# Folding a norm's scale into the QKV weights, reordering the prologue and keying the output projection per tile, in a statically ordered transformer block

## The chip, the cores and the metric

The kernel runs on one core of a Trainium2 chip. The metric is the device time of one execution in microseconds (us). "Faster" or "slower" is given at 2%; differences below that are told with their 95% intervals.

Ratios are the mean time of one kernel's fast runs over that of the kernel before in the same rounds, so they are not quite the ratio of the medians that stand beside them. The experiments ran in three batches (e; f, g and p; c), each with its own runs of the kernel before; between batches it is safer to compare ratios than times.

## The reference, cut to what matters

One transformer block with adaptive layer norms: 2048 tokens, width 1024, 32 query heads of width 32 that share one key and one value head, and a gated feed-forward of width 3584, all in bf16.

```python
mod = (silu(c) @ w_mod).reshape(1, 6, 1, -1)
sa, ca, ga, sb, cb, gb = ...                 # shift, scale, gate of both halves
h = layernorm(x) * (1 + ca) + sa
q = (h @ wq).reshape(heads); k = h @ wk; v = h @ wv        # one k and v for all heads
x = x + ga * (softmax(q @ k.T / sqrt(32)) @ v) @ wo
h = layernorm(x) * (1 + cb) + sb
x = x + gb * (silu(h @ w1) * (h @ w3)) @ w2
```

## The kernel before

The program is a graph of small nodes. A scheduler on the host lays it out with a simple model of durations: at each step it takes the engine that can start first and gives it the ready node of best priority. What goes to the chip is a fixed order for each engine, with semaphores (counters on which one engine waits for another) between the engines. The program has no means of changing this order while it runs. That a group of matmuls is "keyed on" a tile means that it is made to wait for that tile.

The order on TensorE in words: scores (class S) go first, since they feed the exponentials on ScalarE; the products with V and the sums of the denominators (V, D) come next; the rest (class F: projections, feed-forward) fills what is left; it is called filler below.

```python
# Dag.schedule (cut): the choice on TensorE
def key(c):
    s, n = c
    if n.cls == "S":
        r = 0
    elif n.cls is not None:
        r = 1 if att or t - n.est > 1.0 else 4
    else:
        r = 3
    return (r, n.prio, n.seq)
...
st = max(dma_free, s + 1.2)             # the model of a load
dma_free = st + n.nbytes / 300e3
n.vis = dma_free + 0.8
```

Matmuls write into PSUM, from which VectorE or ScalarE must copy the result before the place can be used again (the copy is called eviction). The eight PSUM banks are two general ones (PB) and a ring of six for the scores (SP). The front works in four groups of 512 tokens; each is normalised, transposed on TensorE and evicted with scale and shift, and then gives keys, values and, for the first group, queries:

```python
# ln_transpose (cut): eviction needs the modulation MODC, so all of w_mod's first part must be in
G.add("act", lambda e, ...: e.activation(dst(c), PBH[g.bank][...], ACT.Identity,
      scale=MODC[:, fm, c:c + 1], bias=MODC[:, fs, c:c + 1]), ...)
...
for tb in range(NTB):
    for i in range(4):
        ln_stats(tb * 4 + i)
    ln_scale(tb * 4, 4)
    ...
    ln_transpose(4, q0, ..., 0, 1, ("act", "dve") if tb < 2 else ("dve",))
    kv(tb)                       # keys and values of 512 tokens
    if tb == 0:
        qproj(0, 0)
```

After that come eight blocks of 256 queries, numbered from 0: 128 exponentials of 128x1024 each, then `post`: output projection WO, second norm, and feed-forward. The feed-forward of block b fills TensorE while the scores of block b+1 run.

```python
def post(q0, qn):                # one block: two tiles of 128 tokens
    for i in range(nt):
        t = t0 + i
        for h in range(2):       # WO; keyed on BOTH tiles of QT (qkeys(f, q0, qn))
            g = mm_group(NC, ..., lambda f, s=s: qkeys(f, q0, qn) + [("WOG", f), ("X", s)], prio=4)
            ...
        ln_stats(t, s); ln_scale(t, 1); ln_norm(t, i, s)
        dma(lambda e, t=t, i=i: e.dma_start_transpose(QT[:, :, t * P:(t + 1) * P], xnt(i)), ...)
    for c in range(NC):          # modulate on VectorE
        G.add("dve", lambda e, c=c: e.tensor_scalar(QT[:, c, q0:q0 + qn], ..., ALU.mult, ALU.add), ...)
    # feed-forward: 448 matmuls of 256 columns for w1, w3 and 224 for w2
```

The DMA transpose of the first tile writes that tile's part of QT. Since WO of the second tile is keyed on both tiles, it waits for that transpose, which it does not need.

The softmax here doesn't subtract the row's maximum and nothing guards it: scores larger than these inputs give would overflow.

Of the kernel before, what the change touches and what calls it, by code (L numbers as in the profile page):

```python
# [3 lines left out]
BF16 = mybir.dt.bfloat16  # L4
# [15 lines left out]
class Group:  # L20
    def __init__(self):
        self.bank = None
        self.nodes = []


class Dag:
# [76 lines left out]
    def schedule(self, banks):  # L103
# [41 lines left out]
        while left:  # L145
            best = None
            for e in ENGS:
                if not ready[e]:
                    continue
                tf = t_free[e]  # L150
                fb = free_banks() if e == "pe" else None
                cands = []
                tmin = None
                for n in ready[e]:
                    est = n.est
                    if n.acq is not None:
                        if not fb:
                            continue
                        est = max(est, fb[0][0] + SEM_LAT)
                    if n.cls == "S":  # L160
                        idle = [bank_idle(b) for b in n.sbanks if b not in closed]
                        if any(x is None for x in idle):
                            continue
                        est = max([est] + [x + SEM_LAT for x in idle if x])
                    s = max(tf, est)
                    cands.append((s, n))
                    if tmin is None or s < tmin:
                        tmin = s
                if not cands:
                    continue  # L170
                if best is None or tmin < best[0]:
                    best = (tmin, e, cands)
# [29 lines left out]
            if n.acq is not None:  # L202
                fb = free_banks()
                b = fb[0][1]
                old = bank_group[b]
                if old is not None:
                    for x in old.nodes:
                        if x.eng != "pe":
                            n.deps.append(x)
                bank_group[b] = n.acq  # L210
                n.acq.bank = b
# [19 lines left out]
            if n.dsem is not None:  # L231
                st = max(dma_free, s + 1.2)
                dma_free = st + n.nbytes / 300e3
# [101 lines left out]
def build(nc, x_in, wq_in, wk_in, wv_in, wo_in, w1_in, w3_in, w2_in, c_in, wmod_in, out, S, D, F):  # L335
# [14 lines left out]
    NXS = 8  # L350

# [12 lines left out]
    NG = 2  # L364
    TP = -1
# [17 lines left out]
    RS = sb("RS", [P, NT], F32)  # L383
    NHALF = sb("NHALF", [P, 4], F32)
# [16 lines left out]
    WKK, WVK = [("QT", NC - 1, S - 512), ("QT", NC - 1, S - 384)], [("QT", NC - 1, S - 256), ("QT", NC - 1, S - 128)]  # L401
    SCBK = [("QT", a, S - 512 + b) for a in range(NC // 4) for b in range(0, 512, P)]
# [14 lines left out]
    def grp():  # L417
        return Group()
# [27 lines left out]

    xload(0, 8)
    for k in range(NC):
        dma(lambda e, k=k: e.dma_start(WM01[:, k, :], wmod_in[k * P:(k + 1) * P, 0:2 * D]), ("wm01", k),
            writes=[("UR", k)], nbytes=P * 2 * D * 2)  # L450
    dma(lambda e: e.dma_start(WKV[:, 0], wk_in.rearrange("(c p) f -> p c f", p=P)), "wk", writes=WKK, nbytes=65536)
    dma(lambda e: e.dma_start(WKV[:, 1], wv_in.rearrange("(c p) f -> p c f", p=P)), "wv", writes=WVK, nbytes=65536)
    WQK = [("WREG", "q")]
    dma(lambda e: e.dma_start(WQ[:, :, 0:P], wq_in[:, 0:P].rearrange("(c p) f -> p c f", p=P)), "wq0",
        writes=[("WQ", 0)] + WQK, nbytes=P * D * 2)


    G.add("act", lambda e: e.activation(CT[:], CROW[:], ACT.Tanh, scale=0.5), reads=["CROW"], writes=["CT"], dur=0.25)
    G.add("dve", lambda e: e.scalar_tensor_tensor(CT[:], CT[:], 1.0, CROW[:], ALU.add, ALU.mult),
# [13 lines left out]
    g = grp()  # L473
    for k in range(NC):
        def mm(e, k=k, g=g):
            for j in range(16):
                i = e.matmul(PB[g.bank][:, j:j + 1], WM01[:, k, j * P:(j + 1) * P], SCT[:, k:k + 1],
                             start=(k == 0 and j == 0), stop=True, skip_group_check=True)
            return i
        G.add("pe", mm, reads=["SCT", ("UR", k)], dur=16 * 0.06, lat=0.2, acq=g if k == 0 else None,  # L480
              groups=[(g, "w")], mode="F")
    G.add("dve", lambda e, g=g: e.tensor_copy(MODC[:, 0, :], PB[g.bank][:, 0:8]), writes=[("MODC", 0)],
          groups=[(g, "r")], dur=0.13, prio=0)
    G.add("dve", lambda e, g=g: e.tensor_scalar(MODC[:, 1, :], PB[g.bank][:, 8:16], 1.0, None, ALU.add),
          writes=[("MODC", 1)], groups=[(g, "r")], dur=0.13, prio=0)
    G.add("pool", lambda e: e.tensor_copy(WKR[:], WKV[:, 0].unsqueeze(2).broadcast_to([P, NC, 4, 32])), reads=WKK,
          writes=["WKR"], dur=1.3)

    def ln_stats(t, s=None):
        s, q = t % NXS if s is None else s, t % 4  # L490
        for a in range(2):
# [3 lines left out]
              reads=[("ST", q, 0), ("ST", q, 1)], writes=[("MV", t)], dur=0.15, prio=2)  # L495

# [20 lines left out]
    def ln_transpose(nt, q0, dst, dkeys, fs, fm, engs, prio=5):  # L517
# [3 lines left out]
        for cb in range(NC // ncb):  # L521
            g = grp()
# [9 lines left out]
            for h in range(ncb):  # L532
                c = cb * ncb + h
                en = engs[cb % len(engs)]
                if en == "act":
# [12 lines left out]
    def mm_group(n, f, reads_f, n_cols=512, per=1, prio=5, late=0):  # L548

        g = grp()  # L550
        for i0 in range(0, n, per):
            def run(e, i0=i0, g=g):
                for i in range(i0, min(n, i0 + per)):
# [5 lines left out]
                  groups=[(g, "w")], mode="F", prio=prio)  # L559
        return g  # L560

    def kv(tb):
        sl = slice(tb * 512, (tb + 1) * 512)
        hk = lambda c: [("HT", c, tb), HKEY]
        g = mm_group(NC, lambda e, b, c: e.matmul(b, WKR[:, c].rearrange("p a f -> p (a f)"), HT[:, c, sl],  # L565
                                                  start=c == 0, stop=c == NC - 1), lambda c: ["WKR"] + hk(c))
        G.add("dve", lambda e, g=g: e.tensor_copy(KT[:, sl], PB[g.bank]), writes=[("KT", tb)], groups=[(g, "r")],
              dur=dve_t(512), prio=1)

        def vmm(e, b, i):  # L570
# [3 lines left out]
        g = mm_group(4 * NC, vmm, lambda i: WVK + hk(i % NC), n_cols=128, per=NC)  # L574
        G.add("dve", lambda e, g=g: e.tensor_copy(V[:, tb * 4:tb * 4 + 4, :].rearrange("p t f -> p (t f)"),
                                                  PB[g.bank][:, 0:128]),
              writes=[("V", tb)], groups=[(g, "r")], dur=dve_t(128), prio=1)

    def qproj(tb, f):
        sl = slice(tb * 512, (tb + 1) * 512)  # L580
        g = mm_group(NC, lambda e, b, c: e.matmul(b, WQ[:, c, f * P:(f + 1) * P], HT[:, c, sl],  # L581
                                                  start=c == 0, stop=c == NC - 1),
                     lambda c: [("WQ", min(f, 1)), ("HT", c, tb), HKEY] + WQK)
        G.add("dve", lambda e, g=g: e.tensor_copy(QT[:, f, sl], PB[g.bank]),
              writes=qkeys(f, tb * 512, 512), groups=[(g, "r")], dur=dve_t(512), prio=1)
# [4 lines left out]
    for tb in range(NTB):  # L590
        for i in range(4):
            ln_stats(tb * 4 + i)
        ln_scale(tb * 4, 4)
        q0 = 4 if tb == 1 else 0
        for i in range(4):
            ln_norm(tb * 4 + i, q0 + i)
        if tb + 2 < NTB:
            xl = xload(tb * 4 + 8, 4)
        ln_transpose(4, q0, lambda c, tb=tb: HT[:, c, tb * 512:(tb + 1) * 512],
                     lambda c, tb=tb: [("HT", c, tb)], 0, 1, ("act", "dve") if tb < 2 else ("dve",))  # L600
        kv(tb)
        if tb == 0:
            qproj(0, 0)
    dma(lambda e: e.dma_start(WQ[:, :, P:D], wq_in[:, P:D].rearrange("(c p) f -> p c f", p=P)), "wq1",
        reads=[("WQ", 0)], writes=[("WQ", 1)], nbytes=7 * P * D * 2, after=xl)
    wo_load = dma(lambda e: e.dma_start(WO[:], wo_in.rearrange("(c p) f -> p c f", p=P)), "wo", writes=["WO"],
                  nbytes=D * D * 2, after=xl)
    for f in range(1, NC):
        qproj(0, f)
# [58 lines left out]
    for tb in range(1, NTB):  # L668
        for f in range(NC):
            qproj(tb, f)  # L670
# [5 lines left out]
    def attention(q0, qn):  # L676
# [5 lines left out]
        for f in range(NC):  # L682
            pend = []
            trs = []
            for s in range(ns):
# [19 lines left out]
                G.add("pe", smm, reads=sorted({("KT", kt // 4) for kt in kts}) + qkeys(f, q0, qn),  # L705
# [91 lines left out]
    WKEYS = [("WMS", i) for i in range(3)] + WQK + [("WQ", 0), ("WQ", 1)]  # L797
# [17 lines left out]
    def post(q0, qn):  # L815
        t0, nt = q0 // P, qn // P
        xs = lambda t: t % 4
        G.chain = 1
# [3 lines left out]
        for i in range(nt):  # L822
            t = t0 + i
            s = xs(t)
            for h in range(2):
                g = mm_group(NC, lambda e, b, f, t=t, h=h: e.matmul(  # L826
                    b, QT[:, f, t * P:(t + 1) * P], WO[:, f, h * 512:(h + 1) * 512], start=f == 0,
                    stop=f == NC - 1), lambda f, s=s: qkeys(f, q0, qn) + [("WOG", f), ("X", s)], prio=4)
# [6 lines left out]
            dma(lambda e, t=t, i=i: e.dma_start_transpose(QT[:, :, t * P:(t + 1) * P], xnt(i)), ("xt", i),  # L835
                reads=[("XN", i)], writes=[("QT", c, t * P) for c in range(NC)], nbytes=P * D * 2 * 2)
        for c in range(NC):
            G.add("dve", lambda e, c=c: e.tensor_scalar(  # L838
                QT[:, c, q0:q0 + qn], QT[:, c, q0:q0 + qn], MODC[:, 4, c:c + 1], MODC[:, 3, c:c + 1],
                ALU.mult, ALU.add), reads=[("MODC", 3), ("MODC", 4)] + qkeys(c, q0, qn), writes=qkeys(c, q0, qn),  # L840
                dur=dve_t(qn, 4) + 0.12, prio=2)
# [128 lines left out]
```

## Time and profile before

The time before was 1196.2 us (median of 3; 1194.97 to 1197.2).

The table of windows shows how the execution falls into stages. Its columns are the window, its length, then busy time of TensorE (PE), its weight loads, VectorE (DVE), ScalarE (ACT) and GpSimd (POOL), the granted clock of TensorE, the share of DMA time and GB/s. These are the front, the middle and the end:

```profile
0.00:60.00 60.00, 32.31 (x441) 20.74 (x442) 47.70 (x104) 18.48 (x22) 9.12 (x27) 0.93 0.81 274
...
235.00:1060.00 825.00, 822.66 (x11971) 566.10 (x11969) 723.81 (x1050) 818.07 (x925) 21.36 (x24) 1.00 0.68 187
1060.00:1210.00 150.00, 121.27 (x1193) 101.67 (x1191) 64.48 (x109) 22.61 (x30) 1.58 (x4) 0.96 0.70 189
```

In the middle TensorE is idle for 2.3 us of 825, and ScalarE is busy for 99% too. In the first 60 us TensorE is idle for 27.7.

The timeline of the front (start, duration, engine, line, operation, and in brackets the idle time before it with what ended it):

```profile
20.51 0.59 PE L477 MATMUL PB<-SCT,UREG 128*128 128x1 bf16 x16 [0.97 <-DMA UREG<-in_w_mod_dram]
...
21.41 2.79 ACT L536 ACTIVATE HREG<-SP,MODC 128x512 bf16<-128x512 bf16 x4 [18.98 <-DVE MODC L484]
...
38.05 1.94 ACT L710 ACTIVATE UREG<-SP 128x1024 bf16<-128x1024 f32 x2 [4.37 <-PE SP L700]
```

ScalarE waits 19.0 us for the modulation before it can evict the first transpose. The first exponential (L710) starts at 38.05.

The timeline of the end, from WO of the last tile (L826) to the last feed-forward (L855):

```profile
1096.73 1.89 PE L826 MATMUL SP<-WO,QT 128*128 128x512 bf16 x8
...
1101.72 3.22 PE L889 MATMUL SP<-HREG 128*128 128x256 bf16 x28
...
1106.15 3.31 SPq L835 DMA_TRANSPOSE QT<-XN  x1
...
1112.26 2.14 DVE L838 TENSOR_SCALAR QT<-QT,MODC 128x256 bf16<-128x256 bf16 x8 [5.80 <-DMA QT<-XN]
1114.54 6.46 PE L855 MATMUL PB<-QT,HREG 128*128 128x256 bf16 x32 [9.61 <-DVE QT L838]
```

TensorE has run out of filler (L889, the feed-forward of block 6), waits 9.6 us, and then runs 32 matmuls in 6.46 us; later 32 take 3.49 by the chain of waits. The granted clock, by the windows, is 0.50 from 1114.5 to 1118 and 1.00 from 1121 on.

These are the feed-forward rows of the groups on TensorE in block 4, from its first exponential at 564.24 to the next block's at 691.38 (count, busy us, mean ns, idle before):

```profile
L855 PE MATMUL PB<-QT,WREG 128*128 128x256 bf16 x256 | 32.3, 273 | 0.0
...
L855 PE MATMUL PB<-QT,HREG 128*128 128x256 bf16 x128 | 16.1, 273 | 0.0
L889 PE MATMUL PB<-WREG,HREG 128*128 128x256 bf16 x105 | 14.2, 274 | 0.0
L889 PE MATMUL PB<-HREG 128*128 128x256 bf16 x65 | 8.5, 274 | 0.0
...
L855 PE MATMUL PB<-QT,X 128*128 128x256 bf16 x64 | 8.0, 273 | 0.0
L889 PE MATMUL PB<-X,HREG 128*128 128x256 bf16 x56 | 7.3, 273 | 0.0
```

Blocks are numbered from 0. The counts add up to 674, and to 672 when counted exactly from exponential to exponential. That is one whole block's feed-forward (448 + 224): per block of scores, TensorE gets one block of filler done, without idling.

### The profile page before, as it was taken

The numbers are of one execution on the slowest core, as the hardware profiler recorded it, in microseconds if no ns is written. First come the engines' busy times: TensorE is split into PE (matmuls) and PEld (weight loads), VectorE is DVE, ScalarE is ACT, GpSimd is POOL, SyncE is SP. The second block draws the span as 40 slices with busy tenths as digits, with TensorE's granted clock in tenths as the row PEclk, the third lists the DMA queues.
The fourth block names the chain that finished last, engine by engine and source line by source line (L and its number), as shares of the span: only waits on it lengthen the run. The fifth ranks groups of instructions, "written<-read, shape, count | busy, mean of one in ns | idle before, by whom it ended". The sixth has DMA issues, their size and how long they took to land.

```text
span 1195.7 us, 35104 instructions
## 1 busy us (share of the span) xinstructions
PE 1126.3 (94%) x15681; PEld 757.1 (63%) x15681; DVE 967.2 (81%) x1443; ACT 1021.1 (85%) x1146; POOL 33.7 (3%) x59
## 2 busy tenths in 40 slices
PE   4697996799999999999999999999999999999798
PEld 3343442476666776777577766776677757777687
DVE  7867877788988998898889888989889988994451
ACT  1488999999999999999999999999999999990110
POOL 2000000000010001000000000000100010000000
PEclk9898997899999999999999999999999999999899
DMA  8715007266568665866497557765786558768894
GB/s 304 246 55 177 2 7 180 62 189 167 160 174 233 169 176 139 254 197 169 131 253 198 162 157 209 217 178 142 190 239 177 166 150 248 203 166 233 213 274 130
DMA packets 387446, 212.11 MB, mean 177 GB/s; under 512 B 25824, under 2 KB 379104, under 8 KB 387296
## 3 DMA queue, kind: packets, MB, share of 16 engines
q1 hardware_dynamic: 387296, 209.87, 62.6%
q8 instruction: 123, 2.02, 0.7%
q14 instruction: 27, 0.22, 0.1%
HBM read 201.46 MB, written 4.19 MB: 172 GB/s over the span
## 4 chain that ended last, share of the span: by engine, by line
PE 83%; ACT 8%; DVE 4%; DMA 3%; SPq 1%; issue 0%; POOL 0%
PE PB L855 31%; PE SP L700 12%; PE PB L889 12%; PE PB L741 9%; ACT UREG L710 8%; PE PB L581 4%; PE PB L826 4%; PE SP L889 4%; PE SP L855 3%; PE PB L761 2%; DMA WREG<-in_w_mod_dram 1%; DMA UREG<-in_w_mod_dram 1%; DMA QT<-XN 1%; DVE ST L492 1%; DVE HREG L542 1%; PE SP L565 1%
## 5 line engine op out<-in xcount | busy, mean ns | idle before, releaser
L710 ACT ACTIVATE UREG<-SP 128x1024 bf16<-128x1024 f32 x1024 | 967.9, 1041 | 35.0 <-PE SP L700 31.2
L729 DVE TENSOR_TENSOR UREG<-UREG 128x2048 bf16<-128x2048 bf16 x256 | 311.8, 1218 | 24.8 <-ACT UREG L710 20.8
L700 PE MATMUL SP<-QT,KT 32*128 32x256 bf16 x4096 | 206.9, 277 | 25.3 <-ACT UREG L710 18.9
L724 DVE TENSOR_TENSOR UREG<-UREG 128x2048 bf16<-128x2048 bf16 x128 | 156.5, 1223 | 69.8 <-ACT UREG L710 69.0
L855 PE MATMUL PB<-QT,WREG 128*128 128x256 bf16 x1664 | 211.6, 275 | 0.4 <-DVE QT L838 0.2
L855 PEld LDWEIGHTS PB<-QT,WREG 128*128 128x128 bf16 x1664 | 153.5, 98 | 47.6 <-issue 30.7
L700 PEld LDWEIGHTS SP<-QT,KT 32*128 32x128 bf16 x4096 | 61.0, 92 | 148.2 <-ACT UREG L710 68.9
L855 PE MATMUL PB<-QT,HREG 128*128 128x256 bf16 x1088 | 139.1, 277 | 10.7 <-DVE QT L838 9.6
L741 PE MATMUL PB<-UREG,V 128*32 128x256 bf16 x4032 | 130.5, 275 | 0.5 <-ACT UREG L710 0.5
L855 PEld LDWEIGHTS PB<-QT,HREG 128*128 128x128 bf16 x1088 | 101.3, 99 | 40.9 <-issue 29.0
L741 PEld LDWEIGHTS PB<-UREG,V 128*32 128x32 bf16 x4032 | 98.3, 97 | 25.4 <-issue 18.3
L889 PE MATMUL PB<-WREG,HREG 128*128 128x256 bf16 x700 | 91.2, 273 | 0.4 <-DVE WKR L770 0.4
L864 ACT ACTIVATE GSB<-GSB 128x512 bf16<-128x512 bf16 x56 | 36.5, 652 | 62.3 <-DVE GSB L862 62.3
L889 PEld LDWEIGHTS PB<-WREG,HREG 128*128 128x128 bf16 x700 | 63.8, 98 | 23.3 <-issue 13.3
L855 PE MATMUL PB<-QT,X 128*128 128x256 bf16 x512 | 64.8, 273 | 0.0
L826 PE MATMUL PB<-WO,QT 128*128 128x512 bf16 x232 | 62.9, 396 | 1.0 <-DMA QT<-XN 0.5
L581 PE MATMUL PB<-HREG,WREG 128*128 128x512 bf16 x256 | 62.7, 381 | 0.0
L889 PE MATMUL PB<-HREG 128*128 128x256 bf16 x476 | 62.2, 273 | 0.0
L855 PEld LDWEIGHTS PB<-QT,X 128*128 128x128 bf16 x512 | 46.9, 98 | 13.2 <-issue 8.2
L864 ACT ACTIVATE WREG<-WREG 128x512 bf16<-128x512 bf16 x56 | 36.8, 657 | 21.2 <-DVE WREG L862 21.2
L889 PEld LDWEIGHTS PB<-HREG 128*128 128x128 bf16 x476 | 43.4, 98 | 14.8 <-issue 8.9
L779 DVE RECIPROCAL WKR<-WKR 128x128 f32<-128x128 f32 x48 | 44.5, 940 | 0.3
(109 smaller groups left out, 953.0 us busy)
## 6 DMA issues: line engine op xcount, KB each, us to landing
WREG<-in_B_w_dram SPq DMA_DIRECT2D x112, 512.0 KB, 5.0
HREG<-in_B_w_dram SPq DMA_DIRECT2D x74, 512.0 KB, 5.0
WREG<-in_B_w_dram SPq DMA_DIRECT2D x33, 896.0 KB, 5.2
X<-in_B_w_dram SPq DMA_DIRECT2D x38, 512.0 KB, 4.8
HREG<-in_B_w_dram SPq DMA_DIRECT2D x21, 896.0 KB, 5.1
X<-in_B_w_dram SPq DMA_DIRECT2D x10, 896.0 KB, 5.0
X<-in_A_x_dram SPq DMA_DIRECT2D x32, 256.0 KB, 4.4
WREG<-in_w_mod_dram SPq DMA_DIRECT2D x16, 512.0 KB, 5.2
```

The costliest lines, as they stand in the source:

```text
L581: g = mm_group(NC, lambda e, b, c: e.matmul(b, WQ[:, c, f * P:(f + 1) * P], HT[:, c, sl], start=c == 0, stop=c == NC - 1), lambda c: [("WQ ...
L700: r = e.matmul(SP[:, b, o:o + qn], KT[32 * gg:32 * gg + 32, kts[j] * P:(kts[j] + 1) * P], QT[32 * gg:32 * gg + 32, f, q0:q0 + qn], start=T ...
L710: G.add("act", lambda e, u=u, h0=h0, n=n, b0=b0, nb=nb: e.activation(U[:, u, h0 * W:(h0 + n) * W].rearrange("p (b w) -> p b w", b=nb), SP[ ...
L724: G.add("dve", lambda e, tr=tr, u=u, fu=first_u: e.tensor_tensor(TR[:, tr, 0:4 * W], U[:, fu, 0:4 * W], U[:, u, 0:4 * W], ALU.add), reads= ...
L729: G.add("dve", lambda e, tr=tr, u=u: e.tensor_tensor(TR[:, tr, 0:4 * W], TR[:, tr, 0:4 * W], U[:, u, 0:4 * W], ALU.add), reads=[("TR", tr) ...
L741: r = e.matmul(PB[g.bank][32 * gg:32 * gg + 32, 0:qn], V[:, kt, :], U[:, pu, (gg * npk + j) * qn:(gg * npk + j + 1) * qn], start=w0 + n == ...
L761: r = e.matmul(PB[g.bank][32 * gg:32 * gg + 32, qn:2 * qn], SEL[:, ga, gj, :], TR[:, tr, (gg * npk + j) * qn:(gg * npk + j + 1) * qn], sta ...
L779: G.add("dve", lambda e, h=h, da=da: e.reciprocal(DSB[:, da, h * 128:(h + 1) * 128], DSB[:, da, h * 128:(h + 1) * 128]), reads=[("DSB", da ...
L826: g = mm_group(NC, lambda e, b, f, t=t, h=h: e.matmul(b, QT[:, f, t * P:(t + 1) * P], WO[:, f, h * 512:(h + 1) * 512], start=f == 0, stop= ...
L855: return e.matmul(b[:, j * qn:(j + 1) * qn], w13[:, w, c, j * P:(j + 1) * P], QT[:, c, q0:q0 + qn], start=c == 0, stop=c == NC - 1)
L864: G.add("act", lambda e, b=b: e.activation(TB[b], GS[b], ACT.Tanh, scale=0.5), reads=[("GS", b)], writes=[("TB", b)], clear=alias("TB") if ...
L889: G.add("pe", lambda e, g=g, j=j, fc=fc, hf=hf, first=first, w2s=w2s: e.matmul(PB[g.bank][:, j * 256:(j + 1) * 256], HHT[:, hf * NH + fc, ...
```

## The change

The intent: evict the first transposes without waiting for the modulation, by folding the scale into the weights of Q, K and V and the shift into biases; make all keys first and values later, so that exponentials start early and do not stop; use TensorE instead of DMA for the transposes of the first and the last block; and let WO of a tile wait only for its own tile. The diff is cut and in places shortened. It also changes the model of the loads (300 to 350) and moves the statistics of two tiles to ScalarE.

```diff
-                dma_free = st + n.nbytes / 300e3
+                dma_free = st + n.nbytes / 350e3
...
+                if fs is None:                      # ln_transpose: plain copies
+                    ... e.activation(dst(c), src(), ACT.Identity) / e.tensor_copy(dst(c), src())
...
-    def kv(tb): ...                                 # keys and values together
+    def kproj(t0, n, allow=None): ...               # four column tiles, bias on eviction
+    def vproj(tb): ...
...
+    ORDER = ("w0", "w1", "w2", "w3", "x8", "x9", "w4", "x10", "x11", "w5", "w6", "w7", "q", "x12", ...)
+    ONACT = (3, 6)                                  # statistics of two tiles on ScalarE
+    tr(0, 4, None, ("act", "dve"), (2, 3, 4, 5))    # transposes of tokens 0-1535 before the modulation
+    tr(4, 4, ...); tr(8, 4, ...)
+    ... bias matmuls for Q, K, V; WKV and WQ multiplied by 1 + scale
+    kproj(0, 256, (2,)); qproj(0, 256, 0, (3,)); kproj(256, 256, (0, 1)); ...
+    tr(12, 4, None, TR3E, (0, 1)); kproj(1536, 512, (0, 1))
+    for tb in range(NTB):
+        vproj(tb)
...
+        pet = q0 == 0 or q0 + qn == S
-                    stop=f == NC - 1), lambda f, s=s: qkeys(f, q0, qn) + [("WOG", f), ("X", s)], prio=4)
+                    stop=f == NC - 1), lambda f, s=s, t=t: [("QT", f, t * P), ("WOG", f), ("X", s)], prio=4)
...
+            if not pet:
+                dma(... dma_start_transpose ...)
+        if pet:
+            ln_transpose(nt, 0, ..., 3, 4, PETE[q0 > 0], prio=4)
```

## The prediction

> **What bounds it now.** The table of windows gives three stages. From 230 to 1080 us TensorE is busy over 99% and ScalarE about 98%: both are full, one block of 256 queries takes about 127 us, and the change only reorders WO there. Of 1195.7 us TensorE is busy 1126.3; the 69 idle us are 27.7 in 0-60, 7 in 60-110, 8 in 110-200, about 11 in 200-235, 15 in 1080-1196.
>
> **Front.** Timeline: the last of eight modulation loads releases TensorE at 20.5, the scale is ready at 21.3, and only then can any transpose be evicted (ScalarE waited 19.0 us for it, in the list of waits). The first exponential starts at 38.05; up to 62 only 12 have run, because keys for tokens 512 on come late, behind statistics, evictions and values on VectorE and TensorE. Steady from 62 at about 0.95 us each.
>
> After: evictions of tokens 0-1535 need no scale, so they run under the loads. Four x tiles now come before the end of the modulation weights: 1 MB at the 391 GB/s of 10-20 us is 2.6 us, so the scale comes near 23.8. Then bias matmuls, folding K and the first Q weights (estimate 1.6 us on VectorE), 256 keys, 256 queries, evictions and scores: first exponential near 31. The other keys follow sooner, but eight evictions of the last 512 tokens (0.73 us each, 5.6 us) stay on ScalarE. 16 exponentials should be done near 52, against 65.8 now: 10 to 13 us gained. Added: 56 one-column bias matmuls (34 ns each in the trace, 2 us), folding the other Q weights (estimate 3 us VectorE). The column-tiled key projection costs no more, as the V product shows (64 matmuls of 256 columns in 1.86 us). Waits for modulation loads at 82-110 stay.
>
> **Block 0's end.** Queries run out at 177 and its feed-forward starts at 222.8; the second tile's WO is held until 204.9 though its input exists at 187, since it is keyed on the first tile's DMA transpose. The change shortens this too. In all, front TensorE idle falls by about 16 us, minus 2 to 3 of added work: 13 us gained, as ScalarE permits.
>
> **Tail.** WO of the last tile waits from 1084 to 1096.6 for the same false dependence; filler ends at 1104.9; DMA transpose 1106.15 to 1112.26, modulation 2.15, feed-forward at 1114.5: TensorE idle 9.6 us. Its clock falls, so the first 32 matmuls take 6.46 us instead of 3.49 (the Trainium skill, "TensorE: Matmul & The Clock Gate", Part 1, says idleness throttles the array; this trace agrees). After: both tiles' norms finish near 1095, under the filler; 16 transposes cost about 1 us. Gain 11 to 12 us.
>
> **Sum:** 13 + 11.5, about 25 to 26 us: 1170 us, range 1160 to 1181. Faster over 2% (below 1172.3): 0.57; within: 0.41; slower: 0.02.
>
> **Signs.** First exponential at 29 to 33, steady by 52; TensorE idle in 0-60 near 18 to 20; feed-forward of block 0 starting near 193 to 200; no idle over 2 us before the last feed-forward and its first 32 matmuls near 3.5 us; block period unchanged at 127.
>
> **What would make it wrong.** VectorE (norms, evictions, folding) limits the keys, so exponentials start but stutter; the loads are later than I think; ScalarE, as full as TensorE in the middle, keeps the front gain from passing; waits at 82-110 grow because the schedule now assumes faster loads.

## The result, and the profile after

The changed kernel takes 1183.38 us (median of 4; 1179.25 to 1185.56) against 1195.94 for the kernel before in the same rounds: ratio 0.989, interval 0.9861 to 0.992. The gain is clear of noise, but under the 2% at which a kernel is called faster. I had predicted 1170, with a range from 1160 to 1181. Half of the expected 26 us came.

The windows after, the same three as above:

```profile
0.00:60.00 60.00, 41.17 (x742) 29.47 (x743) 45.11 (x102) 33.90 (x51) 18.38 (x54) 0.86 0.79 275
...
235.00:1060.00 825.00, 812.70 (x11938) 556.01 (x11951) 713.38 (x1045) 819.39 (x927) 17.76 (x24) 1.00 0.66 182
1060.00:1210.00 150.00, 116.19 (x1098) 100.83 (x1098) 57.82 (x97) 12.95 (x22) 1.58 (x4) 0.99 0.73 189
```

The first 60 us have 18.8 us of TensorE idle, as predicted (18 to 20). The middle has 12.3 us of it, where there were 2.3. What these 10 us did to the total is worked out below.

The front after:

```profile
24.06 0.54 PE L656 MATMUL PB<-SCT,UREG 128*128 128x1 bf16 x16
...
26.11 0.11 DVE L666 TENSOR_SCALAR MODC<-PB 128x8 f32<-128x8 f32 x1
...
29.58 0.61 PE L537 MATMUL SP<-IDENT,XN 128*128 128x128 bf16 x4 [0.18 <-DVE XN L523]
30.12 1.90 PE L587 MATMUL SP<-HREG,QT 128*32 128x256 bf16 x32
...
36.22 9.52 ACT L841 ACTIVATE UREG<-SP 128x1024 bf16<-128x1024 f32 x10 [0.50 <-PE SP L831]
```

The first exponential starts only 1.8 us earlier than before, but ten then run without a stop.

The end after:

```profile
1079.74 1.89 PE L958 MATMUL SP<-WO,QT 128*128 128x512 bf16 x7
...
1086.06 0.61 PE L537 MATMUL SP<-IDENT,XN 128*128 128x128 bf16 x8
...
1099.72 3.22 PE L1025 MATMUL SP<-HREG 128*128 128x256 bf16 x28
1102.78 1.91 PE L991 MATMUL PB<-QT,HREG 128*128 128x256 bf16 x16
1104.52 1.91 PE L991 MATMUL SP<-QT,HREG 128*128 128x256 bf16 x16
```

The second tile's transposes run at 1086, over 16 us before the filler (L1025) ends at 1102.9; the last feed-forward (L991) follows at once, and its first 32 matmuls take 3.5 us. The wait of 9.6 us and the slow clock after it are gone. The page "TensorE: Matmul & The Clock Gate" of the Trainium skill, Part 1, says that an idle array is throttled and released after some microseconds of work; both traces agree (6.46 us for 32 matmuls after the pause, 3.5 without one).

And the feed-forward rows of block 4 after, from 554.58 to 680.91:

```profile
L991 PE MATMUL PB<-QT,WREG 128*128 128x256 bf16 x246 | 30.5, 273 | 0.7 <-DVE WREG L1031 0.6
...
L991 PE MATMUL PB<-QT,HREG 128*128 128x256 bf16 x128 | 15.9, 273 | 0.0
...
L1025 PE MATMUL PB<-WREG,HREG 128*128 128x256 bf16 x84 | 11.5, 273 | 0.5 <-DVE WREG L1031 0.5
L991 PE MATMUL PB<-QT,X 128*128 128x256 bf16 x64 | 8.6, 273 | 0.6 <-DVE WREG L998 0.6
L1025 PE MATMUL PB<-HREG 128*128 128x256 bf16 x64 | 8.2, 274 | 0.0
...
L1025 PE MATMUL PB<-X,HREG 128*128 128x256 bf16 x56 | 7.3, 274 | 0.0
```

These are 642 (640 from exponential to exponential), not 672. In block 4 the missing 32 are 3.5 us of work, about what TensorE's idle time (2.6 us) and the shorter block (126.3 instead of 127.1 us) make together. Counted in the same way, block 1 did 43 more than before, and blocks 2 to 7 did 15, 27, 32, 25, 23 and 17 fewer. So after the end of the last exponential 966 are left, where 870 were before. At 0.109 us each (32 in 3.49 us) the 96 more are 10.5 us.

What TensorE waited for in this window (waiter, releaser, us in total, times, longest); before, the same list is empty:

```profile
PE PB L991 <- DVE WREG L1031: 0.6, 1, 0.6
PE PB L991 <- DVE WREG L998: 0.6, 1, 0.6
PE PB L1025 <- DVE WREG L1031: 0.5, 1, 0.5
PE PB L958 <- DVE WKR L901: 0.4, 1, 0.4
PE SP L831 <- ACT UREG L841: 0.4, 1, 0.4
```

One of these waits in the timeline:

```profile
604.19 0.62 PE L892 MATMUL PB<-UREG,SEL 128*32 128x256 bf16 x16
...
604.74 0.72 PE L1025 MATMUL PB<-X,HREG 128*128 128x256 bf16 x5
605.23 0.42 DVE L898 COPY XN<-PB 128x256 f32<-128x256 f32 x1
...
605.56 0.68 DVE L1031 TENSOR_TENSOR WREG<-PB,GBB 128x512 bf16<-128x512 f32 x1
...
606.39 0.93 PE L991 MATMUL PB<-QT,WREG 128*128 128x256 bf16 x7 [0.60 <-DVE WREG L1031]
```

A group of the attention (L892) and a group of the feed-forward (L1025) end within a microsecond of each other, and both are in the two general PSUM banks. VectorE copies out one after the other (L898, then L1031), and TensorE stands until L1031 is done. The page "PSUM — Partial Sum Buffer" of the Trainium skill, in "Engine vs sequencer instructions", says that matmuls start and complete in program order; by that, nothing behind L991 can step in. The list of waits is in keeping with it (0.6 us of idle in a kernel with filler left over), but no run here tests it: the scores that come next, at 607.25, were released by ScalarE only at 607.17.

### The profile page after: what moved, and what is told of

It reads as the page before. It is cut to its first block, busy times and chain, and to the rows that moved or that the text cites. A ratio compares the mean times of both kernels' runs of the same rounds, so it can differ in the third digit from the quotient of the medians.

```text
span 1180.7 us, 35742 instructions
## 1 busy us (share of the span) xinstructions
PE 1125.3 (95%) x15978; PEld 768.7 (65%) x16009; DVE 956.6 (81%) x1440; ACT 1030.2 (87%) x1174; POOL 41.3 (3%) x86
## 4 chain that ended last, share of the span: by engine, by line
PE 67%; ACT 23%; DVE 6%; DMA 2%; POOL 1%; issue 1%; SPq 0%
PE PB L991 22%; ACT UREG L841 21%; PE PB L1025 11%; PE SP L831 9%; PE PB L872 8%; PE SP L991 4%; PE SP L1025 3%; PE PB L608 3%; PE PB L958 3%; PE PB L892 2%; DVE UREG L855 1%; DMA WREG<-in_w_mod_dram 1%; DVE ST L488 1%; DVE UREG L860 1%; ACT GSB L1000 1%
## 5 line engine op out<-in xcount | busy, mean ns | idle before, releaser
L831 PE MATMUL SP<-QT,KT 32*128 32x256 bf16 x4096 | 204.8, 274 | 10.6 <-ACT UREG L841 9.4
L991 PE MATMUL PB<-QT,WREG 128*128 128x256 bf16 x1616 | 201.4, 273 | 2.6 <-DVE GSB L998 0.9
L991 PEld LDWEIGHTS PB<-QT,WREG 128*128 128x128 bf16 x1616 | 148.5, 98 | 45.8 <-issue 30.1
L831 PEld LDWEIGHTS SP<-QT,KT 32*128 32x128 bf16 x4096 | 60.8, 92 | 130.2 <-ACT UREG L841 73.3
L991 PE MATMUL PB<-QT,HREG 128*128 128x256 bf16 x1072 | 133.3, 273 | 1.0 <-DVE HREG L1003 0.6
L872 PEld LDWEIGHTS PB<-UREG,V 128*32 128x32 bf16 x4096 | 102.0, 98 | 25.2 <-issue 16.0
L991 PEld LDWEIGHTS PB<-QT,HREG 128*128 128x128 bf16 x1072 | 98.4, 98 | 28.3 <-issue 17.3
L1025 PE MATMUL PB<-WREG,HREG 128*128 128x256 bf16 x700 | 91.6, 273 | 1.4 <-DVE WREG L1031 1.4
L1025 PEld LDWEIGHTS PB<-WREG,HREG 128*128 128x128 bf16 x700 | 63.4, 98 | 25.1 <-issue 15.9
L991 PE MATMUL PB<-QT,X 128*128 128x256 bf16 x496 | 65.2, 273 | 1.8 <-DVE WREG L998 1.5
L608 PE MATMUL PB<-HREG,WREG 128*128 128x512 bf16 (+1 forms) x303 | 61.6, 342 | 3.6 <-DVE QT L611 0.9
L1025 PE MATMUL PB<-HREG 128*128 128x256 bf16 x504 | 63.9, 273 | 0.0
L958 PE MATMUL PB<-WO,QT 128*128 128x512 bf16 x215 | 55.5, 380 | 3.6 <-DVE X L961 1.9
L991 PEld LDWEIGHTS PB<-QT,X 128*128 128x128 bf16 x496 | 45.3, 98 | 17.4 <-issue 12.8
L1025 PEld LDWEIGHTS PB<-HREG 128*128 128x128 bf16 x504 | 46.5, 98 | 13.0 <-issue 7.4
L509 POOL TENSOR_SCALAR RS<-MV 128x1 f32<-128x1 f32 x32 | 16.1, 506 | 1035.2 <-DVE MV L490 1033.6
```

The costliest lines, as they stand in the source:

```text
L509: G.add("pool", lambda e: e.tensor_scalar(RS[:, t0:t0 + n], MV[:, t0:t0 + n, 1], EPS, None, ALU.add), reads=[("MV", t0 + i) for i in range ...
L608: g = mm_group(NC, lambda e, b, c: e.matmul(b[:, 0:n], WQ[:, c, f * P:(f + 1) * P], HT[:, c, sl], start=c == 0, stop=c == NC - 1), lambda ...
L831: r = e.matmul(SP[:, b, o:o + qn], KT[32 * gg:32 * gg + 32, kts[j] * P:(kts[j] + 1) * P], QT[32 * gg:32 * gg + 32, f, q0:q0 + qn], start=T ...
L872: r = e.matmul(PB[g.bank][32 * gg:32 * gg + 32, 0:qn], V[:, kt, :], U[:, pu, (gg * npk + j) * qn:(gg * npk + j + 1) * qn], start=w0 + n == ...
L958: g = mm_group(NC, lambda e, b, f, t=t, h=h: e.matmul(b, QT[:, f, t * P:(t + 1) * P], WO[:, f, h * 512:(h + 1) * 512], start=f == 0, stop= ...
L991: return e.matmul(b[:, j * qn:(j + 1) * qn], w13[:, w, c, j * P:(j + 1) * P], QT[:, c, q0:q0 + qn], start=c == 0, stop=c == NC - 1)
```

## The experiments

Theory P, formed from these rows: the fixed order of the middle blocks settles into one of a few repeating patterns. In the full one TensorE does 672 feed-forward matmuls per block; in others it does 640 to 650, with waits for PSUM banks, and the rest piles up after the last exponential. Which pattern a kernel gets depends on small things, and the per-tile key of WO is one of them. Rival S: ScalarE is over 99% busy in the middle, so a lead won at the front cannot pass through it.

The counts below are of instructions in the traces; all traces hold all 5376 feed-forward matmuls. The scheduler is part of the program, so the order of each kernel can be laid out and its matmuls counted before it runs; the expectations used that, so a count that came as expected tests the layout and not the theory. The times are the test.

### e1: per-tile key undone

```diff
-  lambda f, s=s, t=t: [("QT", f, t * P), ("WOG", f), ("X", s)]
+  lambda f, s=s: qkeys(f, q0, qn) + [("WOG", f), ("X", s)]
```

> The changed kernel with one line undone: WO of a tile is again keyed on both tiles of its block. Theory P (static pattern): the per-tile key makes the greedy order of the middle blocks settle into a repeating pattern in which TensorE stalls about 2 us per block and does fewer feed-forward matmuls per block, which then pile up after the last exponential. With the old key the idle of TensorE in the middle falls from 12 to below 5 us, the block period goes from 126.3 to about 127.2, feed-forward matmuls per middle block return to 672, and the time is about 1174 us (1170 to 1178), 8 or 9 us faster than the changed kernel. Rival S (ScalarE is full in the middle and cannot pass on the lead): the middle's ScalarE work is the same, so the time stays within 3 us of the changed kernel, 1180 to 1186 us. Rival T (the per-tile key is what made the tail shorter): the time gets worse, about 1188 to 1193 us.

Measured: 1177.91 us (1176.1 to 1180.48, 4 runs; before 1196.74), ratio 0.9844, interval 0.9825 to 0.9862. Blocks 4 to 6 have 672 matmuls each, a period of 127.14 us and no TensorE idle; 870 are left at the end. The rows of block 4 (558.05 to 685.19) that differ most from the changed kernel's, and the window of the middle:

```profile
L991 PE MATMUL PB<-QT,WREG 128*128 128x256 bf16 x256 | 32.3, 273 | 0.0
...
L1025 PE MATMUL PB<-WREG,HREG 128*128 128x256 bf16 x105 | 14.2, 274 | 0.0
...
235.00:1060.00 825.00, 819.54 (x11995) 562.77 (x11993) 721.13 (x1046) 818.23 (x924) 19.39 (x24) 1.00 0.66 184
```

Not all came as theory P had it: blocks 2 and 3 have only 629 and 660, the middle's idle fell to 5.5 us and not below 5, and the gain over the changed kernel is 5.5 us by the medians (4.8 by the means, 3.2 by the profiled spans) and not 8 or 9. The intervals of the two ratios just touch. A cleaner pair came later: c3 and c4 differ in this one line only and ran in the same rounds, at 1181.03 to 1186.39 and 1172.05 to 1175.27 us, so there the per-tile key costs 10.6 us.

The last exponential starts at 1065.7, which is 6.3 us later than in the changed kernel, and yet the kernel is faster. Rival S falls: what counted was not only how early ScalarE finished, but how much filler was left. Nor did the middle hold back the lead: against the kernel before, the 129th exponential of e1 is 4.5 us early and its last one 7.0. Rival T falls too: with the TensorE transposes the tail needs no per-tile key. The order laid out with the per-tile key in the first and last block only is identical to this one on every engine, and with the key in the middle blocks only it is the changed kernel's order; so what e1 undoes is the key's effect in the middle.

### e2, e3, e4: each part alone

e2 is the kernel before with only the per-tile key. e3 is the kernel before with only the TensorE transposes in the first and last block. e4 is the changed kernel with both undone, so the new front alone (`pet = False` and the old key).

> The kernel before with only the per-tile key of WO. My prediction, read as a sum of parts, expects the last tile's WO 12 us earlier and so about 8 to 10 us gained (1186 to 1188 us). Theory P: the wait before the last feed-forward goes (about 10 us), but the middle blocks fall into the stalling pattern (TensorE idle about 2 us per block, period 126.3 to 126.7) and most of it comes back as backlog after the last exponential: 1191 to 1195 us.

Measured: 1190.3 us (1188.32 to 1192.03), ratio 0.9945. Blocks 2 to 6 have 640 to 649 matmuls, 966 are left at the end. The pattern is as theory P had it; the time is 0.7 us under its range, and 2.3 us above that of the sum of parts.

> The kernel before with only the TensorE transposes of the first and the last block, old key of WO. Theory P: the middle keeps its full pattern (idle under 1 us per block, period about 127.2), the wait before the last feed-forward goes from 9.6 us to under 1 us and its first 32 matmuls take about 3.6 us: 1184 to 1188 us. Rival S expects less: the earlier end of block 0 gives ScalarE nothing, but the tail gain of about 10 us is outside the middle, so also 1185 to 1188; this run is there for the sum of parts.

Measured: 1188.08 us (1186.81 to 1191.16), ratio 0.9936: at the upper edge of what was expected. Blocks 4 to 6 have 672 matmuls (blocks 2 and 3 have 629 and 660, with 3.7 and 1.8 us of idle where under 1 was expected), 870 are left, and no wait over 0.1 us stands before the last feed-forward.

> The changed kernel with both changes after attention undone (old key of WO, DMA transposes in all blocks): the new front alone. The prediction's sum of parts expects 13 us gained, 1183 us. Rival S: the lead at exponential 128 is kept, some 6 us gained, about 1188 to 1190 us. Theory P: the front alone moves the blocks into a stalling pattern, TensorE idle 2 to 4 us per middle block, with the backlog after the last exponential above 110 us of TensorE work: 1193 to 1199 us, nothing gained, although exponential 128 starts about 6 us earlier than before.

Measured: 1203.92 us (1202.56 to 1204.43), ratio 1.0058, interval 1.0043 to 1.0073. The new front alone makes the kernel slower, and by more than theory P said. Its 129th exponential starts 4.9 us earlier than before, its last one 6.6 us earlier, but 1109 feed-forward matmuls are left, 239 more than before, or 26 us of work. With that much filler the wait in the tail is gone too, although neither of the two changes that were made for it is in this kernel.

### p1: e1 with DMA transposes again in block 0

```diff
-        pet = q0 == 0 or q0 + qn == S
+        pet = q0 + qn == S
```

> e1_oldkey with TensorE transposes in the last block only; block 0 goes back to DMA transposes. By a sum of parts this costs at most 4 to 5 us of block 0's end (e1 to e4 differ in nothing else at the front), so about 1178 to 1183 us. Theory P: block 0's end sets where the feed-forward stands against the scores, and this one falls into the stalling pattern (600 to 650 feed-forward matmuls per middle block, above 1050 left after the last exponential): 1198 to 1206 us, slower than the kernel before.

Measured: 1203.61 us (1202.09 to 1204.63), ratio 1.0063. A change of the way in which two tiles of the first block are transposed costs 26 us. 239 more matmuls are left than in e1 (1109 against 870), and they have two sources. Block 0's feed-forward starts at 229.4 instead of 213.6, since WO of its second tile again waits for the first tile's DMA transpose (206.1 instead of 194.7); block 1 then gets 445 done where e1 had 524, a third of the difference. The other two thirds are the pattern: 600 in block 2, and 640 to 647 in blocks 3 to 6, where e1 came to 672. In e4 the counts are the same.

### f1 and f2: what bounds the new front

The chain of waits of the changed kernel, between the scale (L666) and the first key projection (L587), reads (start, us, what):

```profile
26.28 1.34 POOL RS L509 x2
27.62 0.54 POOL RS L511
28.16 0.03 issue
28.18 0.55 DVE XN L523
28.73 0.34 DVE QT L698
29.07 0.47 DVE XN L523
29.53 0.05 issue
29.58 0.61 PE SP L537 x4
```

These are norms of later tiles, which stand in the queues before the folding of the K weights (L698) and before the projection. f1 takes the statistics of tiles 8 to 15 away (they use the numbers of tiles 0 to 7; not what the reference asks, although it still passed the comparison, presumably because the tokens have nearly the same statistics). f2 moves loads.

```diff
# f1
     def ln(t):
-        (ln_stats_act if t in ONACT else ln_stats)(t)
-        ln_scale(t, 1)
-        ln_norm(t, t % 8)
+        if t < 8:
+            (ln_stats_act if t in ONACT else ln_stats)(t)
+            ln_scale(t, 1)
+        ln_norm(t, t % 8, None, t % 8)
# f2
-    ORDER = ("w0", "w1", "w2", "w3", "x8", "x9", "w4", "x10", "x11", "w5", "w6", "w7", "q", "x12", ...)
+    ORDER = ("w0", "w1", "w2", "w3", "w4", "w5", "w6", "x8", "w7", "q", "x9", "x10", "x11", "x12", ...)
```

> e1_oldkey with the statistics of tiles 8 to 15 taken away on purpose (they are normalised with the numbers of tiles 0 to 7, so the result is wrong). It frees VectorE of 8 x 1.4 us = 11.5 us and GpSimd of 16 small steps before and around the first exponential; loads and everything else stay. In e1_oldkey the first exponential starts at 36.9 us and the 17th at 60.7. Theory N (after the change the front is bound by the chain of norms on VectorE and GpSimd, not by the loads): first exponential at 31 to 34 us, 17th at 53 to 57. Rival L (the later arrival of the scale bounds it, since four x tiles are loaded before it): both within 1 us of e1_oldkey.

Measured in one look (1171.54 us): the first exponential starts at 32.05 and the 17th at 53.75, against 36.88 and 60.74 in e1. The last modulation load landed at 23.94, as in the changed kernel (23.88). Theory N holds: the statistics of these norms cost the front time, not the loads. How much is less sure, as the 17th exponential lies between 58.4 and 60.8 in the eight traces of kernels with the changed front: 5 to 7 us.

> e1_oldkey with the loads reordered: seven of the eight modulation loads before x tile 8, the eighth and the first Q weights before tiles 9 to 15, so the scale lands about 2 us earlier and tiles 9 to 11 later. Rival L: first exponential about 2 us earlier than e1_oldkey (36.9), near 34.5, and the 17th earlier by as much. Theory N: the first exponential may come up to 3 us earlier too, because norms of tiles 8 to 11 no longer stand before the folding, but their keys come later and the 17th exponential is at 64 us or later against 60.7: the time of the norms is moved, not saved.

Measured in one look (1184.7 us): the last modulation load landed at 22.32. The first exponential starts at 32.30, but the 17th at 65.46, 4.7 us later than in e1. The first exponential came even earlier than either had it (4.6 us before e1's), and the 17th later, as only theory N had it: the norms are moved, not saved.

### g1 and its repetition c4: another number in the scheduler's model

```diff
-  ("wms", sl), writes=wms(sl), nbytes=P * 2048 * 2
+  ("wms", sl), writes=wms(sl), nbytes=P * 2048 * 2 * 2      # both places; only the model reads it
```

> e1_oldkey with one number of the scheduler's model changed: the 512 KB modulation loads for gates and second norm are taken as twice as long when the order is laid out. Nothing else; the program does the same work. In e1_oldkey TensorE and ScalarE stand still in 82 to 113 us for these loads (ScalarE about 7 us). Theory G (the order is laid out for loads that are faster than they are, so TensorE's in-order queue waits for them): ScalarE's idle in 80 to 120 falls to under 3 us, exponential 128 starts 4 us or more earlier than in e1_oldkey (175.0), the middle keeps 672 feed-forward matmuls per block, and the time is 1172 to 1176 us. Rival: the loads themselves are the limit, idle and time stay as in e1_oldkey, 1177 to 1180.

Measured: 1173.15 us (1171.3 to 1174.02), ratio 0.9804, interval 0.9789 to 0.9819. ScalarE's idle between 80 and 120 us fell from 7.9 to 5.3 us by the windows, not below 3. In this trace the 17th exponential already starts 2.3 us earlier than in e1's, and the 129th 4.5 us earlier. The middle is full from block 2 on (672), where e1 had 629 and 660 in blocks 2 and 3; but block 1 has 469 where e1 had 524, and the same 870 are left.

> The same kernel as g1_oldkey_slow_gates, once more on this chip, beside c3, to see whether its lead over e1_oldkey holds: 1171 to 1175 us, ratio to the kernel before 0.979 to 0.982.

Measured: 1172.88 us (1172.05 to 1175.27), ratio 0.98, interval 0.9774 to 0.9826. This version beats both kernels; it is about 10 us faster than the changed one, and against the kernel before it stands on the 2% line.

Its trace settles more of theory G. ScalarE's idle between 80 and 120 is 3.2 us here, the 17th exponential starts only 0.7 us earlier than in e1, and the 129th 4.0 us. So the lead at the 17th is a difference between executions (the orders of e1 and g1, laid out, part only at 84.7 us of the model's time), and the lead of 2.2 us (g1) and 3.3 us (c4) that is won between the 17th and the 129th is that of the changed number. The rival, that the loads themselves are the limit, falls: it had the time at 1177 to 1180. As equally many matmuls are left as in e1, the fuller blocks 2 and 3 add nothing to it.

### c1, c2, c3: the missing combinations

c1 is the kernel before with both changes after attention. c2 is the changed kernel with DMA transposes everywhere. c3 is the changed kernel with g1's number.

> The kernel before with both changes after attention (per-tile key of WO, TensorE transposes in the first and last block), old front. The prediction's view (each of the two takes part of one wait of 10 us in the tail): 1184 to 1187 us. Theory P: the key puts the middle into the 645-matmul pattern whatever the transposes do, so the transposes add nothing to e2_key_alone (1190.3 us): 1188 to 1193 us, slower than the TensorE transposes alone (1188.1) or equal to it; 966 feed-forward matmuls after the last exponential.

Measured: 1190.25 us (1189.75 to 1192.95), ratio 0.9952. The same as the key alone (1190.3). It is 2.2 us worse than the TensorE transposes alone, but the intervals of the ratios overlap, so only "not better" is shown.

> The changed kernel with DMA transposes in all blocks; per-tile key and new front stay. If the TensorE transposes of the last block are what removed the wait of 9.6 us in the tail, this is 5 to 10 us slower than the changed kernel, 1188 to 1193 us. Theory P: with the per-tile key the last transposes land under the filler anyway, the pattern is the same (645 per block, 966 left), and the time is within 3 us of the changed kernel, 1180 to 1186 us.

Measured: 1183.46 us (1182.2 to 1185.62), ratio 0.9892: the changed kernel's time. With the per-tile key the TensorE transposes bring nothing that the medians show (the profiled spans differ by 3.0 us, within the spread of the runs). Either of the two takes the wait out of the tail, and both together do it once.

> The changed kernel with the scheduler's model of the modulation loads doubled, as in g1_oldkey_slow_gates, but with the per-tile key kept. If the better order under those loads were all that g1 gained (4.8 us against e1), this gains as much: about 1178 to 1180 us. Theory P: the middle stays in stalling patterns (640 to 670 feed-forward matmuls per block, about 1000 left at the end) and the gain is given back: 1181 to 1188 us, at least 8 us slower than g1.

Measured: 1183.44 us (1181.03 to 1186.39), ratio 0.9892. The number that brought 5 us with the old key brings nothing with the per-tile key: 641 to 668 in blocks 2 to 6, 993 left.

### The sum that works

One sum accounts for all of these within 1.4 us. Take from each trace the start of the last exponential and the number of feed-forward matmuls that begin after its end. Against before, the time changes by the difference of the first, plus 0.109 us for each matmul more, minus 12.6 us, because in every one of these kernels the wait in the tail (9.6 us) and its slow clock (3.0 us) are gone. The last column is the span of the same profiled run minus that of before (1195.7).

| kernel | last exponential starts | left after it | sum | measured span |
|---|---|---|---|---|
| before | 1072.7 | 870 | | |
| key alone (e2) | 1069.2 | 966 | -3.5 + 10.5 - 12.6 = -5.6 | -5.7 |
| TensorE transposes alone (e3) | 1073.4 | 870 | +0.7 - 12.6 = -11.9 | -11.1 |
| both after attention (c1) | 1066.2 | 966 | -6.5 + 10.5 - 12.6 = -8.6 | -7.8 |
| front alone (e4) | 1066.1 | 1109 | -6.6 + 26.1 - 12.6 = +6.9 | +6.9 |
| front, transposes in last block (p1) | 1062.9 | 1109 | -9.8 + 26.1 - 12.6 = +3.7 | +4.5 |
| front and transposes (e1) | 1065.7 | 870 | -7.0 - 12.6 = -19.6 | -18.2 |
| front and key (c2) | 1063.3 | 966 | -9.4 + 10.5 - 12.6 = -11.5 | -12.0 |
| all (the change) | 1059.4 | 966 | -13.3 + 10.5 - 12.6 = -15.4 | -15.0 |
| all, slow gates (c3) | 1060.1 | 993 | -12.6 + 13.4 - 12.6 = -11.8 | -11.1 |
| e1, slow gates (g1) | 1061.3 | 870 | -11.4 - 12.6 = -24.0 | -23.5 |

The sum is bookkeeping: it says where the time stands, and the experiments say why. The terms move together. A pattern that leaves filler behind lets the scores run ahead, so its last exponential comes early, but it pays more at the end than it gained: the changed kernel against e1 is 6.3 us early and 10.5 us late.

## Why the prediction was wrong

**The middle (the step that failed).** I wrote that "both are full, one block of 256 queries takes about 127 us, and the change only reorders WO there", and added front and tail as if a reordering were free. The reordering moved the middle to another pattern: period 126.3 us, 2 us of TensorE idle per block, and 10.5 us of filler left for the end. Undoing that one line brings 5.5 us (e1), and with another number in the load model 10.6 us (c3 against c4). The sign that I had named, "block period unchanged at 127", failed by 0.8 us and looked like good news. The warning that I gave, that ScalarE "as full as TensorE in the middle, keeps the front gain from passing", was the wrong one: e1 is faster with a later last exponential, and its lead grew from 4.5 to 7.0 us through the middle.

**The parts do not add.** I took the front as worth 13 us by itself. Alone it costs 7 us (e4). With the TensorE transposes it brings 10.2 us (from e3's 1188.08 to e1's 1177.91, whose counts of matmuls per block are the same in every block), because there the pattern is held. So the mechanism was right and the size was a little too large, but only in the presence of another part of the change.

**The front's size.** I expected the first exponential near 31 and the 17th near 52; they came at 36.2 and 59.7. I had timed the way from the scale to the first score by its own operations (7 us) and forgot what else stands in the queues: the scale's matmul was done by 24.6, VectorE got to it at 26.1, and another 10.1 us passed, largely behind norms of later tiles. f1 shows the price of their statistics, 5 to 7 us at the 17th exponential. The saving on evictions was real: from the banks SP, mean 778 ns with scale and shift on ScalarE before, 597 ns without after. The page "ScalarE: Activation LUTs" of the Trainium skill, under "What ACT_TABLE_LOAD costs", gives about 93 ns for each per-partition pointer operand; the difference of 181 ns for two agrees.

**Block 0's feed-forward.** I expected it at 193 to 200; it started at 212.2 (before: 222.8). Of these 10.6 us, 5.9 are the lead of the 129th exponential, and 4.7 a shorter way from there to the feed-forward (38.5 us instead of 43.2). Which part of that way I misjudged was not looked into.

**The tail.** Right: no idle before the last feed-forward, 32 matmuls in 3.5 us, 12.6 us saved by the profiles (I said 11 to 12). Wrong was only the belief that the per-tile key was needed for it: the key and the TensorE transposes are two ways to remove the same wait (c1, c2), and enough filler is a third (e4).

**The total.** Against -13 and -11.5, the terms of the changed kernel are -13.3 for the last exponential, -12.6 for the tail, and +10.5, which my sum did not have. That the first agrees with my 13 is luck: at the 129th exponential the lead was 5.9 us, and the other 7.5 came in the middle, from the filler left behind.

What stays open: why the scheduler's greedy choice locks into one pattern or the other from a given start.

## What to carry to other kernels

In a kernel with a fixed order and two engines that are both nearly full, do not price a change by the idle time at its two ends alone; count how much filler each period of the middle gets done, before and after: some 23 matmuls fewer in each of blocks 2 to 7, which show in the middle only as a TensorE busy share of 98.5 instead of 99.7%, came to 10 us here. Removing a false dependence is not free either: it moves work, and the order that was tuned around it may be lost; test each part of a bundle alone and in pairs. Where the order is laid out on the host, count the filler per period there first. Even the model's own end time would have warned me: laid out from the kernels, it is 1187.4 us for the kernel before, 1172.1 for the changed one and 1164.0 for e1, so 15 us gained and 8 lost to the key, where 12.6 and 5.5 were measured. It is no substitute for a run: for e4 it gives 0.4 us lost where 7 were measured, and it has g1 2 us behind e1.

## What the Trainium skill lacked or had wrong

- "Perfetto Trace Analysis", "Identifying the Most-Contended Engine", ranks engines by occupancy and warns that matmul busy share says little of the distance to the peak; for TensorE it names MFU, the matmul work over the window. Here occupancy hid the loss on ScalarE: it was idle for 0.8 to 1.1 us per middle block in the full and in the stalling pattern alike (blocks 4 to 6 of e1 and of the changed kernel), while the filler done per block was 672 or 640 to 649. The page does not say to take the work done per period of a repeating kernel, where the loss showed.
- The same page, in "Optimization Strategy", speaks of bubbles that repeat on the engine that should be saturated, and names too little PSUM as a possible cause; the waits for the two general banks are in keeping with that. It gives no size for a bubble that matters: here waits of 0.4 to 0.6 us, about five per block, went with 96 deferred matmuls (10.5 us) at the end.
- I found in no page how sensitive a statically laid out order is: one dependence in the middle cost 5.5 us (e1), and the kind of transpose used for two tiles of the first block 26 us (p1 against e1).
- "DMA: Bandwidth & Descriptors" gives a bandwidth for DMA transposes, but I found there no latency for a single tile of 128x1024 between other loads: 3.1 us is the median here, and the last one held VectorE until 6.1 us after its issue (1106.15 to 1112.26).
